# A two-level Strassen product on one core: second pass in written order, S sums on VectorE, GpSimd for outer sums only, and a one-level first group

## The chip, the cores and the metric

One core of a Trainium2 chip. The metric is the device time of one execution in microseconds (us). "Fast" means that a run shows no sign of the slower state that some executions have. TensorE's granted clock is given as a share of full speed; a *half-clock spell* is a time in which it is 0.50.

## The reference

```python
def _attn_ref(q, k, v, g_norm):                   # (8, 8, 576, 64) each
    kv = np.einsum('bhsd,bhse->bhde', k, v)
    out = np.einsum('bhsd,bhde->bhse', q, kv)
    rms = np.sqrt(np.mean(out * out, axis=-1, keepdims=True) + 1e-06)
    return (out / rms * g_norm).astype(np.float32)

def _moe_ref(x, w_tok1, w_tok2, w_ch1, w_ch2):    # x (8, 576, 512)
    h = np.maximum(x.transpose(0, 2, 1) @ w_tok1, 0.0) @ w_tok2
    u = x + h.transpose(0, 2, 1)
    h2 = np.maximum(u @ w_ch1, 0.0) @ w_ch2       # 512 -> 1536 -> 512
    return (u + h2).astype(np.float32)
```

Attention and token mixing (the *first pass*) fill about the first quarter of the time. The *second pass* is channel mixing, the last two products, over nine groups of 512 tokens. The argument is about this second pass.

## The kernel before

The first product of a group (`channel1`) is Strassen's scheme at two levels: seven outer products, each made of seven inner ones. An inner product is six TensorE instructions of 128x128. ScalarE copies the first one to SBUF (`t1`), VectorE adds the others onto it out of PSUM (`u2`, `u3`, quarters of the destination), and whole blocks are added on GpSimd (`padd`). From the blocks a11, a12, a22 come the operands s1 to s4 of the second product (`channel2`, one level, seven products of 24 instructions of 128x256). The sums that make s1 to s4 out of whole blocks are the *S sums*; the texts also call them V sums, as the profile names these tiles `vs`. `uT` is the transposed input, `ps_v` and `ps_w` are the PSUM tiles of the first and the second product, and the *d sums* are sums of the second weight matrix. The program fixes no order: a scheduler orders each engine's queue.

```python
    padd = lambda o, a, b: nc.gpsimd.tensor_tensor(out=o[:, 1:], in0=a[:, 1:], in1=b[:, 1:],
                                                   op=ALU.add)
    def after5():                       # after the fourth outer product
        padd(s3, a22, s1)
        padd(a22, a22, a12)
        relu(a22)
    def after2():
        padd(a11, a11, s2)
        relu(a11)
    def after3():                       # after the sixth
        padd(s3, s3, s4)
        nc.vector.scalar_tensor_tensor(out=s1, in0=s3, scalar=0.0, in1=a22,      # L426
                                       op0=ALU.max, op1=ALU.add)
        nc.vector.scalar_tensor_tensor(out=s3, in0=s3, scalar=0.0, in1=a11,      # L428
                                       op0=ALU.max, op1=ALU.subtract)
        nc.gpsimd.tensor_tensor(out=s2, in0=s1, in1=a11, op=ALU.subtract)        # L430
    def after4():                       # after the seventh
        padd(a12, a12, s4)
        relu(a12)
        nc.gpsimd.tensor_tensor(out=s4, in0=a12, in1=s2, op=ALU.subtract)        # L435
    # ... cut: the plan, and the seven inner products of an outer one
    for g in range(NG):                 # the nine groups; all with two levels
        fetch_u(g + 1)
        for n, outer in enumerate(channel1(g)):
            fill = []                   # in group 0: sums of the weights, woven in
            # ... cut
            weave(outer, fill)
        # ... cut: channel2(g), with the transposes and sums (uT) for the next group between
```

## Time and profile before

| | before |
|---|---|
| median (and range) of 3 runs | 983.84 us (982.23 to 984.05) |
| span of the profiled run, clock | 982.2 us, 0.962 |
| first product of the first group starts at | 261.34 us |
| first group | 88.86 us |
| each later group (start to start) | 78.47 us |
| TensorE work in a later group | 70.8 us |

The starts are read from TensorE's timeline: the first `ps_v` row that follows the `ps_w` rows of a group. TensorE's waits, summed over the run (what waited, for what: us in all, times, longest), show how the lost time is spread:

```profile
PE ps_v L451 <- DVE vs L401: 26.6, 9, 3.0
...
PE ps_v L451 <- DVE u L401: 11.6, 18, 1.0
...
PE ps_v L451 <- DVE uT L191: 6.9, 1, 6.9
PE ps_v L451 <- ACT t L459: 5.9, 9, 0.8
```

The first row is one wait of 3.0 us in each of the nine groups, for an accumulation out of PSUM into a block of s1 to s4 (L401) that stands behind an S sum in VectorE's queue.

### The profile page before, as it was taken

What the parts mean: (1) busy time and instruction counts of PE and PEld (TensorE: products, weight loads), DVE (VectorE), ACT (ScalarE), POOL (GpSimd) and SP (SyncE); (2) the same over time, 40 slices, a digit from 0 to 9 for tenths busy, and PEclk for the clock granted to TensorE, in tenths of its full rate; (3) what the DMA queues carried; (4) which work ended last, traced back from release to release, by engine and by line L of the source; (5) the groups of instructions that cost most, each with busy time, mean ns of one, the idle gap of its engine ahead of it and who ended that gap; (6) DMA issues with size and microseconds to landing.
All of it is one profiled execution on the core that took longest, in us unless ns stands there. A gap on an engine that the chain in (4) does not pass through costs nothing.

```text
span 982.2 us, 12730 instructions
## 1 busy us (share of the span) xinstructions
PE 880.3 (90%) x5262; PEld 741.7 (76%) x5262; DVE 575.1 (59%) x880; ACT 155.4 (16%) x251; POOL 385.9 (39%) x212
## 2 busy tenths in 40 slices
PE   3798979798797998999899899899899899899987
PEld 3565555543397897898799789789789789879976
DVE  2859888799865457256266446446545625626641
ACT  2131221321102001101102101101200110110200
POOL 1544554551635225316306405513522631630640
PEclk9899989899989999999999999999999999999999
DMA  8877778432200020020020011001002002001001
GB/s 271 259 242 247 242 215 296 153 129 96 97 1 1 1 87 1 1 86 1 1 86 2 1 43 43 1 22 65 1 1 86 1 1 86 1 1 43 1 1 43
DMA packets 43577, 72.54 MB, mean 74 GB/s; under 512 B 2688, under 2 KB 21120, under 8 KB 43520
## 3 DMA queue, kind: packets, MB, share of 16 engines
q1 hardware_dynamic: 43376, 71.71, 22.2%
q8 instruction: 41, 0.67, 0.3%
q14 instruction: 16, 0.13, 0.0%
q10 hardware_dynamic: 144, 0.03, 0.0%
HBM read 52.85 MB, written 18.87 MB: 73 GB/s over the span
## 4 chain that ended last, share of the span: by engine, by line
PE 52%; issue 7%; POOL 6%; DVE 3%; ACT 0%; DVEq 0%; POOLq 0%
PE ps_w L507 32%; PE ps_v L451 18%; POOL vs L402 4%; POOL v L402 2%; DVE u L401 1%; PE ps_ut L362 1%; DVE vs L401 1%; ACT t L459 0%; DVE xg L511 0%; DVE vs L428 0%; DVE vs L426 0%; ACT v L404 0%; DVEq L401 0%; POOLq L402 0%
## 5 line engine op out<-in xcount | busy, mean ns | idle before, releaser
L451 PE MATMUL ps_v<-uT,w 128*128 128x128 f32 x1782 | 224.6, 278 | 42.3 <-DVE vs L401 26.6
L451 PEld LDWEIGHTS ps_v<-uT,w 128*128 128x128 f32 x1782 | 210.9, 193 | 49.6 <-DVE vs L401 30.2
L451 PE MATMUL ps_v<-uT,w_ch 128*128 128x128 f32 x864 | 118.1, 278 | 8.7 <-DVE u L401 8.7
L451 PEld LDWEIGHTS ps_v<-uT,w_ch 128*128 128x128 f32 x864 | 107.9, 194 | 13.5 <-DVE u L401 12.3
L507 PE MATMUL ps_w<-w_ch,v 128*128 128x256 f32 x432 | 113.9, 420 | 0.0
L402 POOL TENSOR_TENSOR vs<-vs,v 128x1152 f32<-128x1152 f32 x9 | 23.7, 2629 | 205.6 <-DVE vs L401 205.6
L507 PEld LDWEIGHTS ps_w<-w_ch,v 128*128 128x128 f32 x432 | 89.7, 214 | 13.8
L507 PE MATMUL ps_w<-d,vs 128*128 128x256 f32 x432 | 96.2, 379 | 0.0
L507 PE MATMUL ps_w<-w_ch,vs 128*128 128x256 f32 x432 | 96.2, 379 | 0.0
L402 POOL TENSOR_TENSOR v<-v,vs 128x1152 f32<-128x1152 f32 x27 | 70.9, 2628 | 53.4 <-DVE vs L401 34.2
L507 PEld LDWEIGHTS ps_w<-w_ch,vs 128*128 128x128 f32 x432 | 81.5, 190 | 10.7
L507 PEld LDWEIGHTS ps_w<-d,vs 128*128 128x128 f32 x432 | 80.9, 190 | 10.4
L191 DVE TENSOR_TENSOR uT<-uT 128x512 f32<-128x512 f32 (+1 forms) x72 | 74.6, 1067 | 4.1 <-ACT uT L364 3.3
L401 DVE TENSOR_TENSOR u<-ps_v,t 128x384 f32<-128x384 f32 x63 | 35.1, 557 | 67.7 <-PE ps_v L451 43.2
L459 ACT COPY t<-ps_v 128x384 f32<-128x384 f32 x63 | 30.0, 477 | 276.1 <-PE ps_v L451 265.1
L512 POOL TENSOR_TENSOR xg<-xg,u 128x512 f32<-128x512 f32 x27 | 33.9, 1268 | 97.7 <-DVE u L511 97.7
L250 PE MATMUL ps_kv<-v_in,k_in 128*128 128x128 f32 x320 | 46.2, 308 | 24.9 <-ACT kvp L254 15.6
L250 PEld LDWEIGHTS ps_kv<-v_in,k_in 128*128 128x128 f32 x320 | 43.8, 220 | 32.1 <-ACT kvp L254 18.0
L404 ACT ACTIVATE v<-v 128x1536 f32<-128x1536 f32 x27 | 40.1, 1484 | 164.8 <-POOL v L402 164.8
L401 DVE TENSOR_TENSOR vs<-ps_v,u 128x384 f32<-128x384 f32 x108 | 59.9, 554 | 9.2 <-PE ps_v L451 0.6
L279 POOL TENSOR_TENSOR x<-x,g_sb 128x1024 f32<-128x1024 f32 (+1 forms) x20 | 45.4, 2270 | 48.3 <-DVE x L278 23.4
L511 DVE TENSOR_TENSOR u<-ps_w,u 128x512 f32<-128x512 f32 x18 | 12.4, 691 | 87.0 <-PE ps_w L507 87.0
(81 smaller groups left out, 1116.9 us busy)
## 6 DMA issues: line engine op xcount, KB each, us to landing
qT<-in_q_dram SPq DMA_DIRECT2D x8, 1152.0 KB, 8.0
xg<-u_dram SPq DMA_DIRECT2D x9, 1024.0 KB, 5.5
k_in<-in_k_dram SPq DMA_DIRECT2D x16, 512.0 KB, 4.4
v_in<-in_v_dram SPq DMA_DIRECT2D x16, 512.0 KB, 5.7
u_dram<-x SPq DMA_DIRECT2D x16, 512.0 KB, 3.1
out_dram<-xg SPq DMA_DIRECT2D x16, 512.0 KB, 2.8
raw<-in_moe_w_ch_dram SPq DMA_DIRECT2D x16, 384.0 KB, 5.2
raw<-in_moe_w_ch_dram SPq DMA_DIRECT2D x12, 512.0 KB, 4.6
```

The costliest lines, as they stand in the source:

```text
L191: engine.tensor_tensor(out=o, in0=a, in1=b, op=op)
L250: nc.tensor.matmul(acc[:, i], lhsT=kk[:, j, ts(i, P)], rhs=vv[:, j, ts(i, P)], start=(j == 0), stop=(j == JJ - 1))
L279: nc.gpsimd.tensor_mul(x3, x3, g_sb.to_broadcast([P, n * H, D]))
L362: nc.tensor.transpose(pt[:, c], xg[g][:, i, ts(c, P)], ident)
L401: add = lambda o, ps, x: nc.vector.tensor_tensor(out=o, in0=ps, in1=x, op=ALU.add)
L402: padd = lambda o, a, b: nc.gpsimd.tensor_tensor(out=o[:, 1:], in0=a[:, 1:], in1=b[:, 1:], op=ALU.add)
L404: relu = lambda o: nc.scalar.activation(o, o, AF.Relu)
L451: nc.tensor.matmul(ps[:, w], lhsT=a_of(o, n)[:, ts(w, P)], rhs=uT[g][:, SB[o], SB[n]], start=(start and w == 0), stop=stop, skip_group_che ...
L459: nc.scalar.copy(at["t1"], at["p1"])
L507: nc.tensor.matmul(ps[:, p], lhsT=V[g][n - 1][:, 2 * (s // W) + p, s % W], rhs=w2_of(n)[:, s], start=(start and p == 0 and s == 0), stop=s ...
L511: add = lambda o, ps, y: nc.vector.tensor_tensor(out=o, in0=ps, in1=y, op=ALU.add)
L512: padd = lambda o, a, b: nc.gpsimd.tensor_tensor(out=o, in0=a, in1=b, op=ALU.add)
```

## The change

The intent: keep TensorE busy in the second pass by (1) fixing the order of TensorE, VectorE and ScalarE as written, (2) moving the S sums s2 and s4 from GpSimd to VectorE, (3) leaving GpSimd whole-block outer sums only, and (4) giving the first group a first product of one level, so that the second-level weight sums, and the decoding of the last weights, can come later. The core of the diff:

```diff
+    def keep(ins):
+        return tc.keep_in_program_order(ins) if ordered else ins
+    # tensor_add, relu, copy, matmul: the instructions of before, wrapped in keep()
...
-        padd = lambda o, a, b: nc.gpsimd.tensor_tensor(out=o[:, 1:], in0=a[:, 1:], in1=b[:, 1:],
-                                                       op=ALU.add)
+        padd = lambda o, a, b: tensor_add(o, a, b, engine=nc.gpsimd)
+        relus = []
...
         def after5():
             padd(s3, a22, s1)
             padd(a22, a22, a12)
-            relu(a22)
+            later(a22)                       # appended to relus
...
-            nc.gpsimd.tensor_tensor(out=s2, in0=s1, in1=a11, op=ALU.subtract)
...
         def after4():
-            padd(a12, a12, s4)
-            relu(a12)
-            nc.gpsimd.tensor_tensor(out=s4, in0=a12, in1=s2, op=ALU.subtract)
+            v_sums(s1, s2, s3, a11, a22)     # s1 and s2, on VectorE
+            tensor_add(a12, a12, s4)
+            relu(a12, a12)
+            v_sum3(s3, a11)
+            tensor_add(s4, a12, s2, ALU.subtract)
...
             def third():
                 product(3, "p5", False, True)
                 tensor_add(dst(0, 1), at["p5"], at["u2"])
+                while relus:
+                    relus.pop()()            # the relus of the outer product before
                 after()
...
+    def channel1_once(g):                    # cut: a first product of one level
...
-    cut = 48
+    early, in_group = staggered(weights[:24]), staggered(weights[24:])
+    cut = 38
...
+    ordered.append(True)                     # at the start of the second pass
...
+        if g == 0:                               # cut: a pool for the weights' raw data
+                weave(channel1_once(g), in_group + mix_ch2())
+            sums = [mix_ch1_of(o) for o in ORDER]        # woven into group 0's channel2
```

Also part of the change, and cut above: the blocks of V have another layout, the quarter sums of `channel2` and the d sums move from GpSimd to VectorE too, and in `channel2` the inner product `second` comes third and not fifth.

## The prediction

> **What bounds the kernel now.** I read the page first, then the chain of work that ended last, then the timelines of each engine over one period of the second pass, then the waits of TensorE in the stages ahead of it. The page:
>
> ```profile
> PE 880.3 (90%) x5262; PEld 741.7 (76%) x5262; DVE 575.1 (59%) x880; ACT 155.4 (16%) x251; POOL 385.9 (39%) x212
> PE 52%; issue 7%; POOL 6%; DVE 3%; ACT 0%; DVEq 0%; POOLq 0%
> ```
>
> TensorE is the bound, but not all the time: the chain also runs through GpSimd and through "issue". The chain shows one pattern that repeats every 78.47 us from 350.2 us to the end: eight of the nine groups of tokens, 627.8 of 982.2 us. So a change inside a group counts eight times. One period, TensorE's timeline, from the sixth of the seven outer products on (columns: start, length, engine, line, operation, out<-in, count, idle before it and its releaser):
>
> ```profile
> 451.44 3.51 PE L451 MATMUL ps_v<-uT,w 128*128 128x128 f32 x30
> 455.59 0.94 PE L451 MATMUL ps_v<-uT,w 128*128 128x128 f32 x6 [0.64 <-ACT t L459]
> 456.85 1.60 PE L451 MATMUL ps_v<-uT,w 128*128 128x128 f32 x12 [0.32 <-DVE u L401]
> ...
> 464.06 0.94 PE L451 MATMUL ps_v<-uT,w_ch 128*128 128x128 f32 x6 [0.96 <-DVE u L401]
> 464.83 1.46 PE L507 MATMUL ps_w<-w_ch,v 128*128 128x256 f32 x6
> 469.25 0.94 PE L451 MATMUL ps_v<-uT,w 128*128 128x128 f32 x6 [2.95 <-DVE vs L401]
> 470.02 4.44 PE L507 MATMUL ps_w<-w_ch,v 128*128 128x256 f32 x12
> ```
>
> Undisturbed rates come from start differences: 84 ps_v instructions take 9.38 us (428.66 to 438.04), 0.1117 each; 24 ps_w take 5.18, 0.2158 each; 4 transposes 0.44. A group has 294 ps_v, 168 ps_w and 16 transposes: 32.83 + 36.26 + 1.76 = 70.8 us. The period is 78.47, so **7.6 us of each group are lost**. In start-to-start times: 0.81 and 0.69 at 455 to 458, 1.23 at 464, 3.23 at 469 (each with about 0.1 us of restart), and 1.69 inside the last row, whose 12 instructions take 4.28 us to the next start where 2.59 are due. The windows say why (stretch, length, busy times, clock, DMA):
>
> ```profile
> 467.00:469.20 2.20, 0.00 (x0) 0.00 (x0) 2.20 (x3) 0.00 (x0) 0.11 (x1) 1.00 0.00 0
> 471.00:472.00 1.00, 1.00 (x4) 0.76 (x3) 0.00 (x0) 0.00 (x0) 1.00 (x1) 0.50 0.00 0
> 472.00:473.00 1.00, 1.00 (x4) 0.81 (x3) 0.00 (x0) 0.00 (x0) 1.00 (x1) 0.50 0.00 0
> ```
>
> After the idle stretch the granted clock is 0.50 for about 3.4 us. And the idle stretch itself, from the timelines of VectorE, GpSimd and ScalarE:
>
> ```profile
> 461.78 1.76 DVE L426 SCALAR_TENSOR_TENSOR vs<-vs,v 128x1536 f32<-128x1536 f32 x1 [1.32 <-POOL vs L402]
> 463.93 4.80 DVE L428 SCALAR_TENSOR_TENSOR vs<-vs,v 128x1536 f32<-128x1536 f32 x1
> ```
>
> ```profile
> 451.02 2.63 POOL L402 TENSOR_TENSOR v<-v,v 128x1152 f32<-128x1152 f32 x1
> ...
> 463.68 3.43 POOL L430 TENSOR_TENSOR vs<-vs,v 128x1536 f32<-128x1536 f32 x1 [1.94 <-DVE vs L426]
> ```
>
> ```profile
> 453.69 1.48 ACT L404 ACTIVATE v<-v 128x1536 f32<-128x1536 f32 x1 [4.92 <-POOL v L402]
> 455.08 0.46 ACT L459 COPY t<-ps_v 128x384 f32<-128x384 f32 x1
> ```
>
> Two equal VectorE sums take 1.76 and 4.80 us: the second began while a GpSimd sum ran (463.68 to 467.11) and ended 1.62 us after it. TensorE's accumulations stood behind it in VectorE's queue. The smaller loss at 455 is ScalarE: the relu of a22 waits for GpSimd's sum, and the copy of t that TensorE needs stands behind that relu.
>
> **What the Trainium skill says.** "SBUF — State Buffer", section "Who interferes with whom": a VectorE instruction with two SBUF inputs and a GpSimd instruction that reads SBUF exclude each other for the whole instruction. The trace agrees: 4.80 us against 1.76. "TensorE: Matmul & The Clock Gate", Part 1: the clock is halved after a window of about 3.4 us (free-running) with too little activity. The trace agrees: 0.50 for 3.4 us. The same page, "Engine queue depths": ScalarE, VectorE and GpSimd keep strict order. The trace agrees: the copy at 455.08 waited for an unrelated relu. "VectorE: DVE Perf Modes", section on the TRN2 errata: a float32 tensor_tensor takes (N+151)/0.96 ns, 691 ns for 512[...]; the trace has 689[...]. I use the trace.
>
> **The change in a later group (1 to 8).** The matrix work is the same: 70.8 us. Removed: GpSimd's s2 and s4 sums, and with them the 4.80 us block; the pulling of second-level products in among the last outer products. Moved to VectorE: s2, s4, a12+s4 (1.76 us each), and three quarter sums of 0.69. Changed: GpSimd's six outer sums now cover all 1536 columns, 3.43 us instead of 2.63 (the 1536 row above against the 1152 row). ScalarE takes one more 0.48 us copy per outer product.
>
> I lay this out from the start of the fourth outer product (5) at 0, with 4.69 us per outer product and 5.58 us from its start to GpSimd's first sum (442.73 to 448.31 before). GpSimd: s3 5.58 to 9.01, a22 9.05 to 12.5, a11 12.55 to 16.0. In the compiled order ScalarE's relu(a22) stands before the copy of t of the sixth outer product: relu 12.55, copy 13.95 to 14.4. TensorE has run four products of that outer product by 12.06 and needs the copy: it resumes at 14.45, **2.4 us lost** (0.8 before), plus the same 0.7 behind VectorE. The sixth outer product ends at 17.15; its GpSimd sum s3+s4 runs 17.98 to 21.41. The seventh writes s4 again, so its sum on VectorE must wait for that read, until 21.46, and ends at 22.0; TensorE wanted it at 21.17: **0.9 lost**. It ends at 22.7. Then VectorE does s1, s2, a12, s3, s4 undisturbed; s2 is ready about 4.3 us later, while the first second-level product takes 5.18 us on a11, ready long before. Nothing is lost there. The level sums of the next group's uT end at about 38 us of the 38.0 us second level, just in time.
>
> Lost per group: 2.4 + 0.7 + 0.9 = 4.0 against 7.6, a period of 74.8. The 2.4 + 0.6 us of idleness may again halve the clock, depending on how the free-running window falls; part of that would hide in the 0.9. I add 0.5 us: **75.3, a gain of 3.2 us, 25 us in eight groups.**
>
> **The first group.** One level: 84 pairs of 128x256, 168 x 0.2158 = 36.3 us instead of 32.8. Before, it began at 261.3 with 6.9 us of waiting for uT sums (slowed by GpSimd) and half clock after; start to end of its second level was 88.9 us. Now the uT sums are one level, mostly done in time. But VectorE gets four weight blocks to decode (3.2 us each from its four decode rows, 12.8), eight d sums of 768 (0.95 each, 7.6), and the V sums: per third five sums from PSUM and four in SBUF, 9 x 0.69, 18.6 in all. That is 39 us against 36.3 on TensorE, in strict order, and each decode goes from ScalarE to GpSimd (1.4 us) to VectorE. I lay it out from the group's start at 0, a product being 1.73 us (8 x 0.2158) and a third 12.1. First third: VectorE is ready for decode 1 at 7.8 and gets it at 9.95, ends it at 13.2, and the V sums of this third at 17.4; decode 2 then ends at 21.6 (1 us for GpSimd's lock). Second third: TensorE starts at 12.1 and wants product 4 at 20.7, but the sum u3 that must read the bank first ends at 23.0 (**2.3 lost**); decode 3 follows to 26.2, the a22 sum to 26.9, for which product 3, due at 24.8, waits (**2.2**); end 28.7. VectorE then waits for decode 4 (ScalarE's part stands behind a22's relu) until 29.0, ends it at 32.2, and one d sum and the V sums at 38.7. Last third: product 2 waits for the copy of t behind a12's relu (**0.6**), product 4 for u3, which comes behind two d sums at 42.9 instead of 38.0 (**5.0**). End: 36.3 + 10.1 = 46.4 us, 48 with one spell of half clock. Second level 38. The 28 second-level weight sums (0.55 each, 15.3 us) now lie in VectorE's order there, with the last two batches and the late level-2 sums of uT just before the next group's first accumulation: about 5 us lost once, 1 more in clock. Sum 92 us: **3 us worse** than 88.9.
>
> **The stage ahead.** It loses four decodes (12.8 us) and the 28 sums from VectorE, which is 97% busy in 200 to 250 us (48.66 of 50 in the windows). TensorE's 2.25 us wait at 217.96 and 2.96 at 237.41 on the norm go, by the order of the changed kernel: **5 us gained**, nothing certain.
>
> Sum: 983.8 - 25 + 3 - 5 = 956.8; rounded down, as I laid the waits out at their latest: **955 us**.
>
> **Rivals.** (a) All waits inside a group vanish, TensorE runs solid: 8 x 7.6 = 61 us less, about 925. For it: the chain's big terms are removed. Against: the relu before the copy is in the compiled order, and its wait grows with the 3.43 us sums. (b) Half clock in every group, following the 2.4 us gap: 8 x 1.2 more, about 965. For it: 30% activity in a window was enough before (TensorE active for 1.03 us of 466.9 to 470.3). (c) VectorE becomes the bound of the first group: decode chains and locks against GpSimd's decode sums make it 10 us worse still, 965. Its 39 us against 36 speak for it. (d) The stage ahead gains nothing, since its TensorE is 86% busy in 100 to 200 us: 960.
>
> **Range and chances.** (b), (c) and (d) together reach 975, any one stays at or under 965; part of (a) reaches 938. Eight in ten: 938 to 968. 2% faster is 964.2: 0.80. Within 2%: 0.18. Slower: 0.02, as only slower first-group work without any gain per group would do it.
>
> **What would show it.** Right: a period near 75 us; a TensorE gap near 2.4 us on ScalarE's t copy at the sixth outer product and one under 1 us at the seventh; no VectorE sum of 1536 over 1.8 us in channel 1; GpSimd's sums at 3.43; the first product of the first group 45 to 50 us with gaps on VectorE. Wrong: a period of 71 (then relu order or s4 do not bind), or of 77 and more with 0.50 clock in each group; a first group over 100 us.

## The result, and the profile after

| | before | after |
|---|---|---|
| median of the runs (range) | 983.04 us (981.22 to 984.05) | 942.0 us (941.23 to 948.9) |
| span and clock of the profiled run | 982.2 us, 0.962 | 947.1 us, 0.971 |
| first group starts at | 261.34 us | 253.91 us |
| first group | 88.86 us | 79.72 us |
| second group | 78.46 us | 81.81 us |
| rest, to the end | 553.5 us | 531.7 us |

All outputs are right.

The ratio is 0.9604 (95% interval 0.9562 to 0.9645). Here and below, a ratio is the mean time of one kernel's fast runs over that of the other's of the same rounds, so not quite the ratio of the medians quoted.

The profiled run of the changed kernel was its slowest, at 948.9 us; a repeat later had 940.1 to 942.9 us in three runs and 948.92 in the profiled one. So the trace shows a run some 7 us longer than the usual one. Its parts still add up: 7.4 + 9.1 - 3.4 + 21.8 = 34.9 of the 35.1 us between the two spans.

The page after, busy times and shares of the chain that ended last:

```profile
PE 868.9 (92%) x5136; PEld 737.6 (78%) x5136; DVE 558.9 (59%) x862; ACT 176.3 (19%) x300; POOL 273.0 (29%) x144
PE 63%; DVE 17%; POOL 10%; issue 4%; DMA 3%; ACT 2%; POOLq 0%; SPq 0%; DVEq 0%; ACTq 0%
```

TensorE's share of the chain rises from 52 to 63%. TensorE's waits after:

```profile
PE ps_v L124 <- ACT t L121: 18.1, 8, 2.3
...
PE ps_v L124 <- DVE u L115: 7.4, 9, 2.8
PE ps_v L124 <- DVE vs L115: 5.4, 7, 0.8
```

The 3.0 us waits behind an S sum are gone. In their place stands a wait of 2.3 us in each of eight groups for ScalarE's copy `t`: it was 0.8 before. TensorE's timeline in the fifth of the later groups, sixth and seventh outer products:

```profile
671.37 0.94 PE L124 MATMUL ps_v<-uT,w 128*128 128x128 f32 x6 [2.28 <-ACT t L121]
672.62 1.60 PE L124 MATMUL ps_v<-uT,w 128*128 128x128 f32 x12 [0.32 <-DVE u L115]
...
679.05 0.94 PE L124 MATMUL ps_v<-uT,w 128*128 128x128 f32 x6 [0.80 <-DVE vs L115]
```

ScalarE's timeline at the first of them shows the reason, the relu just ahead of the copy, itself released by a GpSimd sum:

```profile
669.46 1.48 ACT L118 ACTIVATE v<-v 128x1536 f32<-128x1536 f32 x1 [3.88 <-POOL v L115]
670.85 0.46 ACT L121 COPY t<-ps_v 128x384 f32<-128x384 f32 x1
```

Groups lasted 75.04 us where no half clock fell in them, and about 76 where it did, as the windows of two of them show (PEclk is third from the right):

```profile
415.60:491.96 76.36, 73.16 (x480) 68.06 (x480) 40.48 (x57) 13.75 (x22) 20.61 (x6) 0.98 0.08 28
642.96:718.00 75.04, 71.64 (x480) 66.53 (x480) 40.49 (x57) 13.75 (x22) 20.60 (x6) 1.00 0.08 29
```

In the first group, VectorE's timeline has a decode of one weight block at 2.24 us in all (0.43 + 0.69 + 0.43 + 0.69), each row near its undisturbed length:

```profile
263.82 0.43 DVE L157 TENSOR_SCALAR w_ch<-w_ch 128x512 uint32<-128x512 uint32 x1 [2.01 <-POOL w_ch L155]
264.29 0.69 DVE L159 SCALAR_TENSOR_TENSOR w_ch<-raw,w_ch 128x512 uint32<-128x512 uint32 x1
265.01 0.43 DVE L161 TENSOR_SCALAR part<-w_ch 128x512 uint32<-128x512 uint32 x1
265.47 0.69 DVE L163 SCALAR_TENSOR_TENSOR part<-raw,part 128x512 f32<-128x512 uint32 x1
```

### The profile page after: what moved, and what is told of

It reads as the page before. It is cut to its first block, busy times and chain, and to the rows that moved or that the text cites. A ratio compares the mean times of both kernels' runs of the same rounds, so it can differ in the third digit from the quotient of the medians.

```text
span 947.1 us, 12401 instructions
## 1 busy us (share of the span) xinstructions
PE 868.9 (92%) x5136; PEld 737.6 (78%) x5136; DVE 558.9 (59%) x862; ACT 176.3 (19%) x300; POOL 273.0 (29%) x144
## 4 chain that ended last, share of the span: by engine, by line
PE 63%; DVE 17%; POOL 10%; issue 4%; DMA 3%; ACT 2%; POOLq 0%; SPq 0%; DVEq 0%; ACTq 0%
PE ps_w L124 33%; PE ps_v L124 21%; POOL vs L115 5%; POOL v L115 3%; PE ps_kv L266 2%; PE ps_u L345 2%; PE ps_h L327 2%; DVE w_ch L159 2%; PE ps_ut L378 2%; DVE part L161 1%; DVE ms L281 1%; DMA raw<-in_moe_w_ch_dram 1%; DVE x L294 1%; DVE part L163 1%; DVE u L115 1%
## 5 line engine op out<-in xcount | busy, mean ns | idle before, releaser
L124 PE MATMUL ps_v<-uT,w 128*128 128x128 f32 (+1 forms) x1656 | 221.6, 287 | 26.6 <-ACT t L121 18.1
L124 PE MATMUL ps_v<-uT,w_ch 128*128 128x128 f32 (+1 forms) x864 | 126.6, 290 | 5.1 <-DVE u L115 5.1
L115 DVE TENSOR_TENSOR u<-ps_v,t 128x384 f32<-128x384 f32 (+1 forms) x59 | 33.3, 564 | 78.8 <-PE ps_v L124 44.2
L115 DVE TENSOR_TENSOR vs<-ps_v,u 128x384 f32<-128x384 f32 (+1 forms) x99 | 54.9, 561 | 39.8 <-PE ps_v L124 23.5
L121 ACT COPY t<-ps_v 128x384 f32<-128x384 f32 (+1 forms) x59 | 28.4, 481 | 192.1 <-PE ps_v L124 192.1
L118 ACT ACTIVATE v<-v 128x1536 f32<-128x1536 f32 (+1 forms) x30 | 39.4, 1314 | 115.1 <-DVE v L115 83.9
L115 DVE TENSOR_TENSOR v<-ps_v,u 128x384 f32<-128x384 f32 (+1 forms) x78 | 44.3, 568 | 25.1 <-PE ps_v L124 19.9
L345 PE MATMUL ps_u<-h,w_tok 128*128 128x512 f32 x128 | 58.8, 603 | 0.0
L115 POOL TENSOR_TENSOR v<-v,vs 128x1536 f32<-128x1536 f32 x16 | 55.0, 3440 | 10.3 <-DVE v L115 10.3
L327 PE MATMUL ps_h<-x,w_tok 128*128 128x512 f32 x128 | 57.4, 595 | 0.3 <-POOL x L295 0.3
```

Of the source, the lines that this page charges most:

```text
L115: keep(engine.tensor_tensor(out=o, in0=a, in1=b, op=op))
L118: keep(nc.scalar.activation(o, a, AF.Relu))
L121: keep(nc.scalar.copy(o, a))
L124: keep(nc.tensor.matmul(*a, **kw))
L327: nc.tensor.matmul(acc[side, t], lhsT=w_tok1[:, j, ts(t, P)], rhs=x_of(pair, side * J + j), start=(j == 0), stop=False)
L345: nc.tensor.matmul(acc_u, lhsT=w_tok2[:, t, ts(i % J, P)], rhs=h1[i // J][:, t], start=(t == 0), stop=(t == NTOK - 1))
```

## The experiments

There were twelve more runs, of eleven new kernels and the changed one again. "DVE" in a label is VectorE. Each was timed in three rounds beside the kernel before. The times together:

| label | what it is | median us | ratio to before (95%) |
|---|---|---|---|
| b_s_dve | before, s2 and s4 on VectorE | 940.76 | 0.9563 (0.9533 to 0.9593) |
| b_s2_dve | before, s2 alone on VectorE | 941.28 | 0.9586 (0.9569 to 0.9603) |
| b_order | before, second pass in written order | 1083.4 | 1.102 (1.0996 to 1.1044) |
| a_no_order | after, order left to the scheduler | 956.02 | 0.9725 (0.9702 to 0.9748) |
| a_s_pool | after, s2 and s4 back on GpSimd | 966.55 | 0.9836 (0.9809 to 0.9864) |
| a_relu | after, relus behind the next copy of t | 924.85 | 0.942 (0.9391 to 0.9449) |
| a_s4 | after, seventh outer product into another tile | 942.33 | 0.9607 (0.958 to 0.9634) |
| a_relu_s4 | both | 906.59 | 0.9231 (0.9216 to 0.9246) |
| a_best | both, and the first group's sums moved | 905.76 | 0.9223 (0.9209 to 0.9237) |
| a_again | after once more | 942.11 | 0.958 (0.9539 to 0.962) |
| a_ahead | after, all weights decoded ahead | 943.8 | 0.9587 (0.9564 to 0.961) |
| a_two | a_ahead, first group with two levels | 958.46 | 0.9733 (0.9712 to 0.9753) |

My theory after the result was this: the loss of before came from the GpSimd sum of s2, but moving that sum alone would put another sum into VectorE's queue, so the fixed order was needed as well (the queue theory). The *lock* is the exclusion that the prediction describes: a VectorE sum beside a GpSimd sum takes 4.80 us and not 1.76. The rival was that it alone made the loss (the lock theory).

### b_s_dve: the S sums alone

```diff
-            nc.gpsimd.tensor_tensor(out=s2, in0=s1, in1=a11, op=ALU.subtract)
+            nc.vector.tensor_tensor(out=s2, in0=s1, in1=a11, op=ALU.subtract)
...
-            nc.gpsimd.tensor_tensor(out=s4, in0=a12, in1=s2, op=ALU.subtract)
+            nc.vector.tensor_tensor(out=s4, in0=a12, in1=s2, op=ALU.subtract)
```

> The kernel before with only one part of the change: the S sums s2 and s4 move from GpSimd to VectorE, the scheduler still orders. Queue theory (mine): the 4.80 us VectorE sum falls to 1.76, but s2 (1.76) now stands in the same place ahead of the last PSUM sums, so TensorE's 3.13 us gap falls only by about 1.3, and the half-clock spell of 1.7 us may or may not go: a period of 75.5 to 77.2 us, 960 to 973 us in all. Lock theory (the lock with GpSimd is the whole of it): gap and spell both go, period near 74, 945 us. Order theory (only keeping the order matters): no change, 983 us.

940.76 us: the number of the rival; that of my theory was wrong, for a reason that the next run shows. Two words changed in the kernel before give the whole gain of the change. A later group takes 73.68 us, less than the 75.04 of the changed kernel.

### b_s2_dve: one of the two lines

Only the first of the two lines above was edited.

> The kernel before with only the s2 sum (one line) moved from GpSimd to VectorE; s4 stays on GpSimd. The two-line edit (s2 and s4) had a median of 940.8 us. Lock theory (the whole loss of 3.2 us idle plus 1.7 us at half clock per group comes from the one GpSimd sum of s2 at 463.68 that locks the VectorE sum beside it): 941, from 938 to 944, no VectorE sum of 1536 elements over 1.8 us in the last outer product, no TensorE wait on a VectorE V sum, a period of 73.7 us. Rival (s4 on GpSimd has a part in it, by delaying GpSimd's or VectorE's sums of the second level): 950 to 965, with a wait near the second level's start.

941.28 us, a period of 73.67: the one line gives the whole gain. VectorE's timeline in the last outer product, to be held against the 1.76 and 4.80 us rows of before that the prediction shows:

```profile
673.40 1.76 DVE L426 SCALAR_TENSOR_TENSOR vs<-vs,v 128x1536 f32<-128x1536 f32 x1 [1.32 <-POOL vs L402]
675.08 0.55 DVE L401 TENSOR_TENSOR u<-ps_v,u 128x384 f32<-128x384 f32 x1
675.55 1.75 DVE L428 SCALAR_TENSOR_TENSOR vs<-vs,v 128x1536 f32<-128x1536 f32 x1
677.21 1.75 DVE L430 TENSOR_TENSOR vs<-vs,v 128x1536 f32<-128x1536 f32 x1
678.88 0.55 DVE L401 TENSOR_TENSOR vs<-ps_v,u 128x384 f32<-128x384 f32 x1
```

The second sum takes 1.75 us again, and s2 another 1.75. Together they are 1.3 us shorter than the locked sum alone was. And TensorE did not wait for the longer queue, as its timeline of the same time shows:

```profile
676.46 3.19 PE L507 MATMUL ps_w<-w_ch,v 128*128 128x256 f32 x14
679.49 0.94 PE L451 MATMUL ps_v<-uT,w 128*128 128x128 f32 x6
```

Before, the scheduler had put 6 instructions of the second product ahead of this `ps_v` row; here it put 14, just enough to cover VectorE's sums. The queue theory had kept the placement of before in mind, and that placement moved.

So the one line changed two things. Before, the accumulation came 4.72 us after the start of the second sum (463.93, in the prediction):

```profile
468.65 0.55 DVE L401 TENSOR_TENSOR vs<-ps_v,u 128x384 f32<-128x384 f32 x1
```

Here it comes 3.33 us after it (675.55 to 678.88): 3.05 us less for the unlocked sum, 1.66 more for s2, 1.4 us less in all. So the lock's 3.05 us are the size of the wait, 3.13 us (3.23 with the restart), as the lock theory had it; and s2 takes 1.7 us of that back, as the queue theory had it. The eight more instructions ahead of the row cover these 1.7 us (8 x 0.2158), and that neither theory foresaw. What the line would give with the placement of before was not run; by these numbers, an estimate, about 1.7 us of wait would stay in each group.

With the wait gone, the half clock behind it is gone: windows of 73.68 us in b_s_dve have PEclk 1.00. The arithmetic closes: 3.23 us of wait and 1.69 of half clock are 4.9 of the 7.6 us lost in each group, and 78.47 - 73.67 = 4.8.

### b_order: the order alone

`keep()` around the second pass's instructions of the kernel before, nothing else.

> The kernel before with only another part: program order kept in the second pass, nothing else moved; GpSimd keeps its S sums and 1152-column sums. Order theory: most of the gain, 945 to 955 us. Queue theory: the written order of the kernel before puts the relu of a22 ahead of the very next copy of t, the relu of a11 ahead of the one after, and both first V sums ahead of the last outer product's accumulations; laid out by hand TensorE loses about 6, 3.5 and 5 to 8 us per group there, plus half-clock spells: a period of 86 to 94 us, slower than before, about 1045 to 1105 us.

1083.4 us, a period of about 89.1, within the range of the queue theory. TensorE waits long for `t`, as its timeline and ScalarE's show:

```profile
566.45 2.93 PE L458 MATMUL ps_v<-uT,w_ch 128*128 128x128 f32 x12 [5.29 <-ACT t L466]
```

```profile
564.54 1.48 ACT L411 ACTIVATE v<-v 128x1536 f32<-128x1536 f32 x1 [9.57 <-POOL v L409]
565.93 0.46 ACT L466 COPY t<-ps_v 128x384 f32<-128x384 f32 x1
```

In the text of the kernel before, the relu stands right behind the GpSimd sum that feeds it and ahead of the next copy. In written order the copy stands behind it, and TensorE waits 5.3 us. The scheduler had been placing this well; the order is no gain in itself.

### a_no_order and a_s_pool: each main part undone

a_no_order lets `keep()` return its instruction unchanged:

```diff
-        return tc.keep_in_program_order(ins) if ordered else ins
+        return ins
```

> The changed kernel with the scheduler free to reorder, all else as changed. By its compiled order VectorE gets the V sums s1, s2 and s3 in between the last outer product's PSUM sums again, none of them locked. Queue theory: about 2.5 us lost there in place of 0.8, the 2.3 us on ScalarE as in the changed kernel: a period of 76.5 to 78, about 955 to 965 us. Lock theory: the order adds nothing, 942 us. Order theory: all the gain lost, 980 us.

956.02 us, 14 more than the changed kernel. Its later groups take 76.3 to 77.6 us, and the wait for `t` is the same 18.1 us in eight; TensorE's waits for VectorE's `u` rise from 7.4 to 15.0 us in all. These waits alone do not make up the 14 us, as those for `vs` (5.4 us) are gone; six of its eight later groups also have a half-clock spell. So for the changed text the order is worth some 14 us, while for the old text it cost 100.

a_s_pool puts s2 and s4 of groups 1 to 8 back on GpSimd, in the fixed order:

```diff
-        tensor_add(s2, s1, a11, ALU.subtract)
+        tensor_add(s2, s1, a11, ALU.subtract, nc.gpsimd if V_POOL else nc.vector)   # V_POOL: not group 0
...
-            tensor_add(s4, a12, s2, ALU.subtract)
+            tensor_add(s4, a12, s2, ALU.subtract, nc.gpsimd)
```

> The changed kernel with s2 and s4 of groups 1 to 8 back on GpSimd, order kept. s2 (3.43 us) now competes with VectorE's two-input sums a12+s4 and s3, and is needed by the second product of the second level, 5.6 us after its first began. Queue theory with the lock: s2 arrives at 7.8 to 9.5 us after that beginning, 2.2 to 3.9 us late, perhaps with a half-clock spell: a period of 77.3 to 80.6, 960 to 987 us. If the lock were not what counts, s2 would be 0.4 us late: 946 us. Order theory: 942 us.

966.55 us, 24.5 more than the changed kernel. The lock shows the other way round, first in GpSimd's timeline, then in TensorE's:

```profile
454.21 4.82 POOL L116 TENSOR_TENSOR vs<-vs,v 128x1536 f32<-128x1536 f32 x1 [3.99 <-DVE vs L422]
```

```profile
459.08 5.45 PE L125 MATMUL ps_w<-d,vs 128*128 128x256 f32 x24 [1.66 <-POOL vs L116]
```

This time VectorE's sum began first (453.98, 1.75 us) and GpSimd's 3.44 us sum became 4.82. The product of `channel2` that reads s2 waits for it (13.7 us in eight groups). By an estimate from these rows the lock is most of this wait: unblocked, 3.44 us from 454.21 end at 457.65 and not at 459.03. As the order is fixed here, this is the cleaner test of the lock: only s2 and s4 change their engine, and nothing is placed anew.

Half clock falls in each later group too, but not behind this wait. In this group it comes before it, right after the wait for `t` that ends at 441.86, as the window shows:

```profile
442.70:446.10 3.40, 3.08 (x15) 2.99 (x15) 1.50 (x4) 1.97 (x2) 0.61 (x1) 0.50 0.00 0
```

So it is in seven of the eight groups. Of the 24.5 us, then, 13.7 are the wait for s2; why half clock falls in every group here, and how much of the rest it makes, is not shown.

### a_relu and a_s4: the two waits that are left

a_relu holds the relus of a22 and a11 back until the next outer product's copy of t has been written:

```diff
                 product(1, "p1", True, False)
                 copy(at["t1"], at["p1"])
+                while ready:
+                    ready.pop()()
...
-                while relus:
-                    relus.pop()()
+                ready.extend(relus)
+                relus.clear()
```

> The changed kernel with the relus of a22 and a11 emitted one copy of t later, so that no copy of t stands behind a relu that waits for GpSimd. Queue theory: the 2.3 us gap and the 0.7 behind it go, but the sixth outer product now ends 3 us sooner while GpSimd's a11 and s3 sums do not, so the wait of the seventh for s4 grows from 0.8 to about 2.0: a period of 72.8, 18 us less than the changed kernel, about 924 us. Rival (ScalarE's copy was waiting for TensorE anyway): no change, 942.

924.85 us, a period of 72.88 at full clock. ScalarE's timeline has the copy ahead of the relu now:

```profile
437.38 0.48 ACT L121 COPY t<-ps_v 128x384 f32<-128x384 f32 x1 [0.49 <-PE ps_v L124]
438.46 1.48 ACT L118 ACTIVATE v<-v 128x1536 f32<-128x1536 f32 x1 [0.59 <-POOL v L115]
```

The whole wait for t went, but part came back: TensorE's wait in the seventh outer product grew from 0.8 to 1.8 us, because TensorE now arrives earlier at the same GpSimd sum:

```profile
442.48 0.94 PE L124 MATMUL ps_v<-uT,w 128*128 128x128 f32 x6 [1.78 <-DVE vs L115]
```

a_s4 takes this other wait away. The seventh outer product writes into s2's free tile, not into s4's, which a GpSimd sum still reads; the names are exchanged downstream:

```diff
+        V[g][2], V[g][5] = s2, s4
...
-            v_sums(s1, s2, s3, a11, a22)
-            tensor_add(a12, a12, s4)
+            v_sums(s1, s4, s3, a11, a22)
+            tensor_add(a12, a12, s2)
...
-            tensor_add(s4, a12, s2, ALU.subtract)
+            tensor_add(s2, a12, s4, ALU.subtract)
...
-                3: (s4, do(padd, s3, s3, s4)), 4: (s4, after4)}
+                3: (s4, do(padd, s3, s3, s4)), 4: (s2, after4)}
```

> The changed kernel with the seventh outer product written into the tile of s2, which is free, in place of s4, which GpSimd is still reading; the V sums take the tiles crosswise. Queue theory: only the 0.8 us wait goes: a period of 74.2, 936 us. Rival (the wait is for VectorE's queue, not for the tile): no change.

942.33 us, no gain, so the expectation failed. The wait did go: TensorE's waits have no `vs` row any more. But the windows say where its 0.8 us went:

```profile
634.25:709.37 75.12, 72.85 (x479) 67.99 (x478) 40.57 (x57) 13.67 (x22) 20.61 (x6) 0.98 0.09 29
```

The group is as long as an undisturbed one of the changed kernel (75.04), but its clock is 0.98: all six groups from 408.63 to 859.58 us have one half-clock spell each, where the changed kernel had few. The wait for the tile was traded for time at half clock, which comes right after the wait for `t`, still there at 2.3 us.

### a_relu_s4 and a_best: both waits, and the first group

> Both edits. Queue theory: nothing is left to wait for in a group, a period of 70.8 us, which is TensorE's own time; 34 us less than the changed kernel and no half-clock spells, 904 to 910 us. If the two waits hid a third, the period stays above 71.5.

906.59 us, faster than both kernels. With no gap left there is no half clock, and a group is TensorE's own work:

```profile
475.84:546.70 70.86, 70.86 (x479) 66.32 (x478) 40.58 (x57) 13.78 (x22) 20.59 (x6) 1.00 0.09 31
```

The gains show that the waits are not independent: 17 us for a_relu, none for a_s4, 35 for both.

a_best also moves the first group's weight sums: the d sums away from its last third and the second-level batches towards the front of channel2.

```diff
-                weave(channel1_once(g), in_group + mix_ch2())
+                steps, mixes = channel1_once(g), mix_ch2()
+                weave(steps[:14], in_group)
+                for step in steps[14:19]:
+                    step()
+                weave(steps[19:], mixes[:4])
...
+            sums = [mixes[4:] + sums[0], sums[1] + sums[5], sums[2] + sums[6],
+                    sums[3], sums[4], [], []]
```

> Both edits, and in the first group: the d sums leave the places ahead of the accumulations, and the last two batches of weight sums of its second level move to earlier steps where VectorE idles. Expected: the 2.8 us gap at the start of group 1 and its half clock go (4 us), and most of the 2.3 + 1.5 us in the last third of the first group: 7 us less than with both edits, about 900 us.

905.76 us: too little, a miss of about 6 us. The second group's wait went, from 73.90 to 70.84 us, but the first group grew from 79.76 to 80.69, with two waits for `u` (2.4 and 1.7 us) in its first product, and it started 1.2 us later. It is the fastest kernel by its median; its lead over a_relu_s4 is within the intervals.

### a_again, a_ahead and a_two: scatter, and the first group

> The changed kernel again, for a second profile: 941 to 949 us. The first profile took 947.1 us, other runs 939.5 to 943.5. If half-clock spells make the difference, this profile has a mean clock nearer 0.98, and periods of 75.03 us where no spell falls and 75.7 to 76.4 where one does.

942.11 us. The profiled run was again a long one (948.92). Half clock lengthened its second and fifth later groups (76.38 and 75.94 us), where the first trace had it in the second and third (76.36 and 75.97). So the spells vary between runs of the same program; the periods are as expected, but the clock of this profile, 0.973, was not nearer 0.98.

a_ahead decodes all 28 weight blocks in the first pass:

```diff
-    early, in_group = staggered(weights[:24]), staggered(weights[24:])
-    cut = 38
+    early, in_group = staggered(weights), []
+    cut = 48
```

> The changed kernel with all 28 weight blocks decoded in the stage ahead, as before, none in the first group. Theory: VectorE gets 9 us more in the stage ahead (4 x 2.24), and the first group begins 2 to 4 us later than 253.9; its first product takes 37 to 38 us in place of 41.7: about the same time, 938 to 944 us. Rival (the decodes were what held the stage ahead): the first group begins as late as before, at 261, and the time is 946.

943.8 us. The first group is 5.3 us shorter (74.38), starts 2.3 us later (256.19; the starts of kernels with the same first pass spread over 3.5 us, see below), and the total is the same within 2 us: where these four blocks are decoded matters little.

a_two is a_ahead with two levels in the first group, its weight sums woven in as in the kernel before.

> As the run before it, and the first group with two levels like the others, its weight sums woven in as in the kernel before, in program order. Theory: TensorE's own work in that group falls by 3.4 us, but the 20 to 28 weight sums and the eight d sums stand in VectorE's queue within the first product: 5 to 10 us more than with one level, 945 to 952 us. Rival (one level costs, as it is more TensorE work): 3 us less.

958.46 us, 14.7 more than a_ahead: slower as expected, but by more. TensorE's timeline in its first group shows two of several waits behind VectorE:

```profile
277.90 0.94 PE L124 MATMUL ps_v<-uT,w_ch 128*128 128x128 f32 x6 [3.48 <-DVE u L115]
...
295.31 0.94 PE L124 MATMUL ps_v<-uT,w_ch 128*128 128x128 f32 x6 [3.48 <-DVE u L115]
```

Its first group takes 90.95 us. So the one-level first group is worth its extra TensorE work, as this order of sums goes.

## Why the prediction was right or wrong

The direction and the range were right. The predicted time was 13 us too high.

- **The lock behind the 4.80 us sum and the half clock after it: right.** In b_s2_dve one line removes both, and 41 us with them. The lock's 3.05 us are the size of the wait of 3.13 us; but the line gives all of it only because the scheduler placed eight more instructions ahead, which cover the 1.7 us that s2 adds on VectorE. a_s_pool shows the lock in fixed order.
- **"Lost per group: 2.4 + 0.7 + 0.9", a period of 74.8, or 75.3 with half clock: right.** Measured gaps 2.28 (and 0.32) and 0.80 us; 75.04 without and about 76 with half clock. The chain relu, copy, TensorE was read correctly from the compiled order, and a_relu shows that it was the cause. For groups 1 to 8 in the traced run, the 6.8 us that the second group was longer than 75.04 set aside, the gain is 632.0 - (613.5 - 6.8) = 25.3 us; 25 were predicted.
- **The first group: wrong size.** The step that failed is "four weight blocks to decode (3.2 us each from its four decode rows, 12.8)". Those mean durations came from the first pass. There, in the trace of before, every decode row of 128x512 that took more than 0.7 us (up to 2.7) ran beside a GpSimd instruction, and those beside none took at most 0.69. In the first group a block took 2.24 us. The late sums came earlier: TensorE waited 0.8 us in the second third and 2.3 in the last, where 4.5 and 5.6 were laid out. The first product took 41.7 us (253.91 to 295.62), not "46.4 us, 48 with one spell", though it had such a spell (291.5 to 294.9 us). The second level took 38.0 us as predicted. So "3 us worse" was 9.1 us better in the first group.
- **The second group's stall, "about 5 us lost once, 1 more in clock": nearly right in sum.** That group was 6.8 us longer than 75.04. The wait itself was 2.8 us and not 5; the rest was half clock after it and in the t gap. a_best, without it, shows the second group at 70.84.
- **The stage ahead, "5 us gained, nothing certain": 7.4 measured** (261.34 to 253.91). VectorE's busy time from 200 to 250 us fell from 48.66 to 33.33 us, and TensorE's rose from 44.79 to 49.52. Where the first pass and the order were left as in the changed kernel, this start varied from 250.42 (a_s4) to 253.92 us (a_again), so 7.4 is the low end.
- The traced run is thus explained. The first two groups together were 9.1 - 6.8 = 2.3 us better and not 3 worse (5.3), the stage ahead gave 2.4 more, the groups 0.3 more: from the sum of 956.8 this makes 948.8, and 948.9 was measured. **The other 7 us, from 948.9 to the median of 942.0, were not traced,** since both profiles of this kernel fell on its longest runs. Their clock was 0.978 to 0.980 for 0.971 and 0.973, so fewer half-clock spells are the likely cause; this is argued, not shown.

Of the rivals, (a), no wait at all, did not come about in the changed kernel, though a_relu_s4 shows what it would have been: 906.59. Rival (b), half clock in each group, held for some groups only; a_s4 shows that it can hold for all. Rival (c) fell, as VectorE was busy for 30.6 of the 41.7 us. Rival (d) fell too. (The prediction's "(b), (c) and (d) together reach 975" is a slip: its own 10, 10 and 5 on 955 make 980.)

What the prediction did not see is the most useful result: the gain of the S sums needed no fixed order. The scheduler placed TensorE's instructions anew around the moved sum. In the later groups (1 to 8) b_s2_dve gains 38.1 us, the traced run of the changed kernel 18.5. The changed kernel falls short there by 19.6 us: 1.4 us in each of eight groups (11), the second group's 6.8, and two half-clock spells (2.3). The stage ahead and the first group (16.6 us together, against 4.8) make up for much of it. That the totals, 941.28 and 942.0, agree is coincidence.

## What to carry to other kernels

When two equal rows of one engine differ in length (1.76 and 4.80 us), look for the other engine that ran beside the longer one, and try moving that one instruction first: here one line, with the placement that the scheduler then chose, was worth as much as the whole rewrite. Then look for what else moved: without the new placement, about 1.7 of the 3.1 us of each wait would have stayed (an estimate). An order fixed by hand is only as good as the text: check each shared queue for a slow, uncritical instruction (a relu that waits for another engine) ahead of a short, critical one. And do not take an instruction's cost from a mean over stages in which it was locked; take the rows of a quiet stretch.

## What the Trainium skill lacked or had wrong

- "TensorE: Matmul & The Clock Gate", Part 1, gives the half clock "after ≥1 idle window (~3.4µs)", and its table "Why this matters for your kernels" advises no idle gaps over about 3 us. Here shorter gaps did it: 2.95 us in all groups of before (TensorE active for 1.05 us of the 3.4 before the spell, in the group of the prediction); 2.3 us in some groups of the changed kernel, and in all later groups of a_s4. A gap of 1.78 us in a_relu did it in none. The page states no threshold of activity, and the runs only bracket it. Its free-running window agrees with the runs: the same program had groups of 75.04 and of 75.9 to 76.4 us, and in a_s4's record of the clock the spells of the eight later groups begin 75.1 us apart. But it doesn't say what follows for a loop: 22 windows of its 3413 ns are 75.09 us, an estimate from the page's figure, so that a group of 75.04 us meets the window at nearly the same point each time, and a spell may be in all groups or in none. That this is why a_s4 had it in all is not shown.
- "SBUF — State Buffer", "Who interferes with whom", says that the later engine waits for the whole instruction, and the runs agree in both directions. It gives no length for the blocked instruction. Here it was its own length plus what was left of the other: 3.43 - 0.25 + 1.76 = 4.94 against 4.80 measured (VectorE blocked, before), and 1.75 - 0.23 + 3.44 = 4.96 against 4.82 (GpSimd blocked, a_s_pool).
- None of the pages used here warns that a profile's mean durations contain the time for which such a lock held the instruction: the decode row at L163 (128x512) has a mean of 985 ns over the changed kernel's 14 instructions, and 0.69 us in its quiet first group.
